# One Mish activation in bursts of four FFN groups, attention's small operations on DVE, and an engine order written by hand from the third unit on

## The chip, the cores and the metric

The kernel runs on one core of a Trainium2 chip. The core has a matrix engine (PE, whose weight loads are shown as PEld), a vector engine (DVE), an activation engine (ACT), a general engine (POOL) and a queue engine (SP) that issues the DMAs here. The metric is device time in microseconds (us); the time of a kernel is the median over its runs. The profile is of one execution, and its span runs from the first to the last instruction.

## The reference

Queries, keys and values have the shape 4 batches x 8 heads x 768 tokens x 64. Each key is compared only with queries of the same hash bucket (the signs of six projections). The attention output, as 3072 tokens x 512, goes through a feed-forward layer (FFN) with the Mish activation.

```python
mask = q_bucket[:, :, :, None] == k_bucket[:, :, None, :]
scores = scale * np.matmul(q, k.transpose(0, 1, 3, 2))
scores = np.where(mask, scores, -1000000000.0)
scores = scores - np.max(scores, axis=-1, keepdims=True)
attn = np.exp(scores)
attn = attn / (np.sum(attn, axis=-1, keepdims=True) + 1e-09)
...
h = x @ w_in                      # 512 -> 2048
sp = np.where(h > 20.0, h, np.log1p(np.exp(np.minimum(h, 20.0))))
g = h * np.tanh(sp)               # Mish
return (g @ w_out).astype(np.float32)   # 2048 -> 512
```

## The kernel before, in words

Every operand of a matmul is held as two float16 parts, a high and a low one, each scaled by a power of two; a product is three matmuls (high x high, high x low, low x high). The weights come as 64-bit floats and are taken apart on the chip.

The work goes by *units* of 256 tokens of one batch, three to a batch, twelve in all. A unit has eight *slots* of attention (`n` = 0 to 95): one pair of heads (`j`, or `hh` for one head of it) and 128 of the tokens. It also has eight *groups* of the FFN (`m` = 0 to 95): 256 hidden columns each. Group `m` is worked on 10 slots behind slot `n` (`OFF`).

A slot runs through `att_scores` (8 matmuls `ps`, both heads in PSUM, two tiles in all), `att_max` (DVE, negated maximum of each head), `att_scale` (POOL: `sc`, then `bi`), `att_exp` (ACT, two exponentials `p` with their sums; three `p` tiles in all), `att_recip` (POOL `rt`, DVE reciprocal `rv`), `att_hi` (POOL, high part of the normalised weights, tile `hl`, three in all), `att_lo` (DVE, low part, then an SP DMA that transposes `hl` into `PTt`). Every second slot has `att_pv` (36 matmuls `pv`, the product with V) and `att_x` (high part on ACT, low part on DVE, into `X`).

A group runs through `ffn_h` (24 matmuls into `h`), `ffn_a` (ACT: a scaled copy `hs`, an exponential), `ffn_m` (DVE minimum), `ffn_r` (ACT: square, logarithm, exponential), `ffn_g` (DVE), `ffn_g2` (POOL, high and low part) and `ffn_out` (12 matmuls into two sums `o`, one for each 128 tokens). After the eighth group the sums are copied out and stored. `h`, `pv` and the small hash and statistics matmuls share two PSUM tiles (`acc`).

In the last unit of a batch the next batch's keys and values are loaded, split, hashed and transposed; every unit does that for the next unit's queries (`kvL`, `kvS`, `kvM`, `kvK`, `kvH`, `kvV`, and `q` in their place: load, square sum, scale, split, hash, values).

Until slot 25 a scheduler orders the instructions of each engine by a model of their times. From slot 26 on (`MAN0`) each engine follows the program's order, which a string sets, one letter for a step. S is scores, x maximum, c scale, E exponentials, C reciprocal, I and 0 and 1 the high and low parts; H, A, M, R, G, g, O are the FFN's steps, V and X the product with V:

```python
OFF, STEP0, STEP1 = 10, 'SCxgIH0cAV1GEMXORP', 'SCxgIH0cAV1GEMXOmhsRklP'
LAGS = (0, 0, 0, 0, 1, 1, 1, 1, 0, 0, 0, 0, 1, 2, 2)
```

Of the kernel before, what the change touches and what calls it, by code (L numbers as in the profile page):

```python
# [29 lines left out]
def lsh_attention_mish_ffn(  # L30
# [31 lines left out]
    nc.scalar.preload_act_table_set("natural_log_exp_and_others")  # L62

# [738 lines left out]
```

## Time and profile before

| what | value |
|---|---|
| runs shown | 988.99 us median of 3 (987.65 to 990.5) |
| profiled execution: span | 984.3 us, 17525 instructions |
| profiled execution: its own time | not listed apart; the median stands 4.7 us above the span |
| PE busy | 814.6 us (83%) |
| DVE busy | 704.6 us (72%) |
| POOL busy | 704.1 us (72%) |
| ACT busy | 685.1 us (70%) |
| mean granted PE clock | 0.956 |

Rows with `|` are groups: line, engine, operation, output<-input, shapes and count, then busy us and mean ns of one, then the idle time of the engine ahead of them and who ended it. `x<-y` with a name behind the arrow is a wait: the instruction on the left waited for the one on the right, with us in total, times and the longest. Rows that begin with two numbers are a start and a duration in us. A row `A:B` gives each engine's busy time in that stretch. In a row with three numbers and slashes these are the least, the median and the largest ns. Matmuls are pipelined: the next starts before the last has ended, so PE's work is read from start to start.

### The profile page before, as it was taken

What the parts mean: (1) busy time and instruction counts of PE and PEld (TensorE: products, weight loads), DVE (VectorE), ACT (ScalarE), POOL (GpSimd) and SP (SyncE); (2) the same over time, 40 slices, a digit from 0 to 9 for tenths busy, and PEclk for the clock granted to TensorE, in tenths of its full rate; (3) what the DMA queues carried; (4) which work ended last, traced back from release to release, by engine and by line L of the source; (5) the groups of instructions that cost most, each with busy time, mean ns of one, the idle gap of its engine ahead of it and who ended that gap; (6) DMA issues with size and microseconds to landing.
All of it is one profiled execution on the core that took longest, in us unless ns stands there. A gap on an engine that the chain in (4) does not pass through costs nothing.

```text
span 984.3 us, 17525 instructions
## 1 busy us (share of the span) xinstructions
PE 814.6 (83%) x6470; PEld 530.7 (54%) x6470; DVE 704.6 (72%) x1169; ACT 685.1 (70%) x1136; POOL 704.1 (72%) x793
## 2 busy tenths in 40 slices
PE   1254567678878999999788999998889999999997
PEld 0132245355545666666455666665555666666664
DVE  5769968897687777776777777777776777777421
ACT  4646778656756867778675778687677677777674
POOL 3589978867777776767887767768886767676522
PEclk9996679889999999999999999999999999999999
DMA  7998695465886655567796565667975555544200
GB/s 216 285 217 189 192 220 163 99 134 103 172 168 132 151 119 124 134 158 182 165 187 130 132 149 129 130 162 168 178 177 134 124 130 128 126 106 119 65 23 22
DMA packets 432693, 143.75 MB, mean 146 GB/s; under 512 B 402912, under 2 KB 423392, under 8 KB 432608
## 3 DMA queue, kind: packets, MB, share of 16 engines
q1 hardware_dynamic: 432608, 142.65, 64.0%
q8 instruction: 50, 0.82, 0.4%
q14 instruction: 35, 0.29, 0.1%
HBM read 35.65 MB, written 6.29 MB: 43 GB/s over the span
## 4 chain that ended last, share of the span: by engine, by line
POOL 39%; issue 15%; PE 13%; ACT 10%; DVE 7%; DMA 3%; POOLq 0%; SPq 0%; ACTq 0%; DVEq 0%
POOL hl L470 11%; POOL ffb L566 7%; POOL sv L437 7%; ACT p L445 6%; POOL sv L438 5%; POOL ffb L565 4%; POOL rt L452 2%; PE h L532 2%; PE h L533 2%; PE h L534 2%; PE o L580 2%; PE o L581 2%; PE ps L422 2%; PE o L582 2%; PE pv L501 1%
## 5 line engine op out<-in xcount | busy, mean ns | idle before, releaser
L445 ACT ACTIVATE p<-ps,sv 128x768 f32<-128x768 f32 x192 | 188.3, 984 | 109.2 <-POOL sv L438 103.2
L486 DVE SCALAR_TENSOR_TENSOR hl<-p,sv,hl 128x768 f16<-128x768 f32 x175 | 227.1, 1330 | 51.1 <-POOL hl L470 50.9
L422 PE MATMUL ps<-KT,QT 128*128 128x512 f16 (+1 forms) x768 | 165.4, 348 | 84.1 <-ACT p L445 73.8
L532 PE MATMUL h<-X,wi 128*128 128x256 f16 x768 | 212.7, 277 | 11.8 <-DVE hsum L328 5.4
L533 PE MATMUL h<-X,wi 128*128 128x256 f16 x768 | 212.4, 277 | 0.0
L534 PE MATMUL h<-X,wi 128*128 128x256 f16 x768 | 212.1, 276 | 0.0
L432 DVE TENSOR_REDUCE sv<-ps 128x1 f32<-128x768 f32 x192 | 175.7, 946 | 20.6 <-PE ps L422 20.4
L470 POOL TENSOR_SCALAR hl<-p,sv 128x768 f16<-128x768 f32 x178 | 167.6, 951 | 10.5 <-DVE sv L453 3.5
L422 PEld LDWEIGHTS <-QT 128*128 128x128 f16 x768 | 75.9, 101 | 153.9 <-issue 107.1
L580 PE MATMUL o<-wo,ffb 128*128 128x512 f16 x384 | 147.5, 384 | 9.2 <-POOL ffb L565 8.5
L582 PE MATMUL o<-wo,ffb 128*128 128x512 f16 x384 | 144.3, 380 | 6.8 <-POOL ffb L566 6.8
L581 PE MATMUL o<-wo,ffb 128*128 128x512 f16 x384 | 146.9, 382 | 0.0
L452 POOL TENSOR_SCALAR rt<-sv 128x2 f32<-128x2 f32 x96 | 38.6, 402 | 123.5 <-ACT p L445 120.3
L541 ACT ACTIVATE ffb<-h,cnegFalse 128x512 f32<-128x512 f32 x88 | 60.1, 684 | 90.8 <-PE h L534 85.9
L566 POOL TENSOR_TENSOR ffb<-ffb 128x512 f16<-128x512 f32 x96 | 113.3, 1181 | 7.7
L501 PE MATMUL pv<-PTt,VT 128*64 128x256 f16 x1728 | 110.0, 281 | 6.0 <-DMA PTt<-hl 5.5
L437 POOL TENSOR_SCALAR sv<-sv,sig 128x2 f32<-128x2 f32 x96 | 93.9, 978 | 21.3 <-DVE sv L432 17.3
L501 PEld LDWEIGHTS <-VT 128*64 128x64 f16 x1728 | 94.7, 113 | 19.6 <-issue 14.1
L565 POOL TENSOR_SCALAR ffb<-ffb 128x512 f16<-128x512 f32 x96 | 63.7, 663 | 45.3 <-DVE ffb L558 31.8
L533 PEld LDWEIGHTS <-wi 128*128 128x128 f16 x768 | 76.3, 99 | 25.0 <-issue 13.7
L532 PEld LDWEIGHTS <-wi 128*128 128x128 f16 x768 | 76.3, 99 | 20.7 <-issue 1.9
L558 DVE SCALAR_TENSOR_TENSOR ffb<-ffb 128x512 f32<-128x512 f32 x96 | 66.6, 694 | 23.4 <-ACT ffb L553 23.4
(217 smaller groups left out, 1287.3 us busy)
## 6 DMA issues: line engine op xcount, KB each, us to landing
out_dram<-ffb SPq DMA_DIRECT2D x24, 256.0 KB, 2.1
stg<-in_k_dram SPq DMA_DIRECT2D x12, 384.0 KB, 3.9
stg<-in_v_dram SPq DMA_DIRECT2D x12, 384.0 KB, 4.3
stg<-in_q_dram SPq DMA_DIRECT2D x9, 512.0 KB, 4.7
wo<-in_moe_w_out_dram SPq DMA_DIRECT2D x8, 512.0 KB, 4.7
wi<-in_moe_w_in_dram SPq DMA_DIRECT2D x7, 512.0 KB, 4.1
PTt<-hl SPq DMA_TRANSPOSE x192, 3.4
stg<-in_moe_w_in_dram SPq DMA_DIRECT2D x5, 512.0 KB, 6.2
```

The costliest lines, as they stand in the source:

```text
L422: nc.tensor.matmul(ps[:, c0 * P:c1 * P], QT[u][:, sl, qi], KT[b, j][:, sl, hh * NCH + c0:hh * NCH + c1].rearrange("p c t -> p (c t)"), sta ...
L432: nc.vector.tensor_reduce(out=d["mneg"][:, hh:hh + 1], in_=d["ps"][hh][:, :S], axis=AX.X, op=ALU.max, negate=True)
L445: nc.scalar.activation(pt, d["ps"][hh][:, :S], AF.Exp, bias=d["bi"][:, hh:hh + 1], scale=d["sc"][:, hh:hh + 1], accum_out=d["sm"][:, hh:hh ...
L470: nc.gpsimd.tensor_scalar(out=hl[:, 0], in0=d["p"][hh], scalar1=rv, scalar2=1.0, op0=ALU.mult, op1=ALU.mult)
L486: nc.vector.scalar_tensor_tensor(out=hl[:, 1], in0=d["p"][hh], scalar=d["rv"][:, hh:hh + 1], in1=hl[:, 0], op0=ALU.mult, op1=ALU.subtract)
L501: nc.tensor.matmul(pv[hh * D:(hh + 1) * D, 0:256], vt[:, w, hh * NCH + c], pt[:, hh, a * NCH + c].rearrange("p s t -> p (s t)"), start=(x ...
L532: nc.tensor.matmul(o, wh, X[:, 0, c], start=(c == 0), stop=False)
L533: nc.tensor.matmul(o, wh, X[:, 1, c], start=False, stop=False)
L534: nc.tensor.matmul(o, wl, X[:, 0, c], start=False, stop=(c == NCC - 1))
L566: nc.gpsimd.tensor_tensor(out=g[:, 1], in0=d["hs"], in1=g[:, 0], op=ALU.subtract)
L580: nc.tensor.matmul(OB[u][s], gh, wo[:, g, 0, f2], start=first, stop=False)
L581: nc.tensor.matmul(OB[u][s], gh, wo[:, g, 1, f2], start=False, stop=False)
```

## The change

The FFN's activation becomes one ACT pass with the Mish function, `ffn_mish`, straight from PSUM. Mish and the exponential lie in different activation tables, so that ACT needs a table load between them. The program now goes by *blocks* of four slots and four groups: in each block the four groups' `ffn_h` and `ffn_mish` come as a burst, and then the four slots' exponentials. There are 44 loads in ACT's order: one at the start, and two in each of 21 blocks, and one for the last burst. The FFN now follows 12 slots behind (`LAG` of three blocks). Its high part is a POOL pass (`ffn_hi`) and its low part a DVE pass (`ffn_lo`). `sc`, `bi` and `rt` move from POOL to DVE. From slot 12 on one of a slot's two high parts moves from POOL to ACT (`lo_pool` 5). The order of each engine is the program's from block 6 on, which is slot 24. The stores get a step of their own (`ffn_store`), and the casts ahead of the statistics matmuls too (`kvD`, `qD`, `bD`). The first unit's groups are summed in two segments instead of three.

```diff
-    nc.scalar.preload_act_table_set("natural_log_exp_and_others")
+    nc.scalar.preload_act_table_set("exp_and_others")
...
+    def act_set(kind, ins):
+        other = latest.get("mish" if kind == "exp" else "exp")
+        if other is not None and not manual[0]:
+            tc.add_manual_dep(ins.ins, other.name,
...
-        nc.gpsimd.tensor_scalar(out=d["sc"], in0=d["mneg"], scalar1=HALF, scalar2=d["sg"], op0=ALU.is_le, op1=ALU.mult)
-        nc.gpsimd.tensor_tensor(out=d["bi"], in0=d["mneg"], in1=d["sc"], op=ALU.mult)
+        nc.vector.tensor_scalar(out=d["sc"], in0=d["mneg"], scalar1=HALF, scalar2=d["sg"], op0=ALU.is_le, op1=ALU.mult)
+        nc.vector.tensor_tensor(out=d["bi"], in0=d["mneg"], in1=d["sc"], op=ALU.mult)
...
-        nc.gpsimd.tensor_scalar(out=t, in0=d["sm"], scalar1=1e-9, scalar2=2.0 ** -PT, op0=ALU.add, op1=ALU.mult)
+        nc.vector.tensor_scalar(out=t, in0=d["sm"], scalar1=1e-9, scalar2=2.0 ** -PT, op0=ALU.add, op1=ALU.mult)
...
+            if lo_pool(n, hh) == 5:
+                nc.scalar.activation(hl[:, 0], d["p"][hh], AF.Copy, scale=rv)
...
-    def ffn_a(m):
-        u, g = divmod(m, NG)
-        ps = FB[m]["ps"]
-        hs, t = ffb[:, ring(m)], ffb[:, 3 + ring(m)]
-        nc.scalar.activation(hs, ps, AF.Copy, scale=CNEG[u == 0][:, g:g + 1])
-        nc.scalar.activation(t, hs, AF.Exp, scale=ES[u // NU, u == 0][:, g:g + 1])
...
-        nc.vector.tensor_scalar(out=t, in0=t, scalar1=E20, scalar2=None, op0=ALU.min)
...
-        nc.scalar.activation(t, t, AF.Square, bias=one_c)
-        nc.scalar.activation(t, t, AF.Ln, bias=one_c)
-        nc.scalar.activation(t, t, AF.Exp, bias=ln2_c, scale=-1.0)
...
+    def ffn_mish(m):
         d = FB[m]
+        d["m"] = ffb[:, m % 3]
+        act_set("mish", nc.scalar.activation(d["m"], d["ps"], AF.Mish, scale=HS[d["key"]][:, d["g"]:d["g"] + 1]))
...
+    def ffn_hi(m):
...
+        nc.gpsimd.tensor_scalar(out=d["p"][:, 0], in0=d["m"], scalar1=GS[d["key"]][:, d["g"]:d["g"] + 1], scalar2=1.0,
+                                op0=ALU.mult, op1=ALU.mult)
...
+    def ffn_lo(m):
...
+        nc.vector.scalar_tensor_tensor(out=d["p"][:, 1], in0=d["m"], scalar=GS[d["key"]][:, d["g"]:d["g"] + 1],
+                                       in1=d["p"][:, 0], op0=ALU.mult, op1=ALU.subtract)
...
-    MAN0 = 26
...
+    LAG = 3
+    MAN0 = 6
...
+    def block(blk):
+
+        n, m = 4 * blk, 4 * (blk - LAG)
...
+        pv(2 * blk - 2)
+        ffn(ffn_h, 0)
+        tail(-1)
+        ffn(ffn_mish, 0)
+        ffn(ffn_h, 1)
+        lows(-1)
+        ffn(ffn_hi, 0)
+        ffn(ffn_mish, 1)
+        head(0)
+        ffn(ffn_lo, 0)
+        prep(n, "mh")
+        ffn(ffn_h, 2)
...
+        ffn(ffn_h, 3)
+        ffn(ffn_hi, 2)
+        ffn(ffn_mish, 3)
+        ffn(ffn_lo, 2)
+        exps(0)
+        prep(n, "skdlP")
+        ffn(ffn_hi, 3)
+        ffn(ffn_out, 0, 0)
+        ffn(ffn_out, 0, 1)
+        ffn(ffn_out, 1, 0)
+        for x in range(1, 4):
+            tail(x - 1)
+            head(x)
+            exps(x)
+            if x == 1:
+                ffn(ffn_lo, 3)
+            lows(x - 1)
+            if x == 2:
+                pv(2 * blk - 1)
+            prep(n + x, "mhskdlP")
+            if x == 1:
+                ffn(ffn_out, 1, 1)
+                ffn(ffn_out, 2, 0)
+                ffn(ffn_out, 2, 1)
+            elif x == 2:
+                ffn(ffn_out, 3, 0)
+            else:
+                ffn(ffn_out, 3, 1)
```

In a block, `tail(x)` is reciprocal and high parts of slot x, `lows(x)` its low parts, `head(x)` scores, maximum and scale; -1 is the last slot of the block before. An output is now given in halves, `ffn_out(group, 128 tokens)`, six matmuls each.

ACT in the middle of the kernel before; `p` is an exponential, `h` an FFN group, `X` the attention output:

```order
L510 ACTIVATE X_5843<-pv_6473,xf_5672 128x256
L551 ACTIVATE ffb_86<-ffb_86,one_c_76 128x512
L552 ACTIVATE ffb_86<-ffb_86,one_c_76 128x512
L553 ACTIVATE ffb_86<-ffb_86,ln2_c_78 128x512
L541 ACTIVATE ffb_86<-h_6559,cnegFalse_2038 128x512
L542 ACTIVATE ffb_86<-ffb_86,es_5676 128x512
L445 ACTIVATE p_6593,sv_6547<-ps_6537,sv_6547 128x768
L445 ACTIVATE p_6595,sv_6547<-ps_6542,sv_6547 128x768
```

and ACT in a block of the changed kernel, from the last slot's exponentials on (`hl` is a high part):

```order
L458 ACTIVATE p_9213,sv_9208<-ps_9198,sv_9208 128x768
L458 ACTIVATE p_9215,sv_9208<-ps_9203,sv_9208 128x768
L524 ACTIVATE X_8823<-pv_9228,xf_7872 128x256
L474 ACTIVATE hl_9297<-p_9215,sv_9208 128x768
L550 ACT_TABLE_LOAD
L550 ACTIVATE ffb_82<-h_9267,hs_7876 128x512
L550 ACTIVATE ffb_82<-h_9300,hs_7876 128x512
L550 ACTIVATE ffb_82<-h_9349,hs_7876 128x512
L550 ACTIVATE ffb_82<-h_9377,hs_7876 128x512
L458 ACT_TABLE_LOAD
L458 ACTIVATE p_9405,sv_9343<-ps_9333,sv_9343 128x768
L474 ACTIVATE hl_9433<-p_9407,sv_9343 128x768
```

Five passes of a group between two slots' exponentials have become four Mish passes between two table loads, and a high part stands ahead of the next slot's exponentials.

DVE for one slot of the kernel before; the names are those of the steps above:

```order
L453 RECIPROCAL sv_5924<-rt_6019 128x2
L432 TENSOR_REDUCE sv_6018<-ps_6008 128x1
L432 TENSOR_REDUCE sv_6018<-ps_6013 128x1
L486 SCALAR_TENSOR_TENSOR hl_6026<-p_5970,sv_5924,hl_6026 128x768
L486 SCALAR_TENSOR_TENSOR hl_6028<-p_5972,sv_5924,hl_6028 128x768
L558 SCALAR_TENSOR_TENSOR ffb_86<-ffb_86 128x512
L547 TENSOR_SCALAR ffb_86<-ffb_86 128x512
L511 SCALAR_TENSOR_TENSOR X_5843<-pv_6062,xf_5672,X_5843 128x256
```

and for one slot of a block of the changed kernel:

```order
L465 TENSOR_SCALAR rt_4470<-sv_4429 128x2
L466 RECIPROCAL sv_4429<-rt_4470 128x2
L428 TENSOR_SCALAR sig_4477<-HKV_1918,hqf_3934 128x1
L447 TENSOR_REDUCE sv_4489<-ps_4479 128x1
L447 TENSOR_REDUCE sv_4489<-ps_4484 128x1
L452 TENSOR_SCALAR sv_4489<-sv_4489,sig_4477 128x2
L453 TENSOR_TENSOR sv_4489<-sv_4489 128x2
L500 SCALAR_TENSOR_TENSOR hl_4473<-p_4434,sv_4429,hl_4473 128x768
L500 SCALAR_TENSOR_TENSOR hl_4475<-p_4436,sv_4429,hl_4475 128x768
L525 SCALAR_TENSOR_TENSOR X_3805<-pv_4502,xf_2854,X_3805 128x256
```

Three 128x2 operations have come to DVE, two of them between the maxima and the low parts, and the FFN's two passes have gone from this place.

More of the change, by code (lines that the diff above doesn't have):

```diff
@@ L515, in lsh_attention_mish_ffn @@
     FB, OB = {}, {}
-    SEGS = ((0, 4), (4, 6), (6, NG))
-    accs = [ffb[:, 2], ffb[:, 5]]
-    def ring(m):
-        return m % 2 if m < NG + 2 else (m - NG) % 3
+    SEGS = ((0, 4), (4, NG))
     def ffn_h(m):
@@ L596, in lsh_attention_mish_ffn @@
-    TOT_U = B * NU
-    MAN0 = 26
-    OFF, STEP0, STEP1 = 10, 'SCxgIH0cAV1GEMXORP', 'SCxgIH0cAV1GEMXOmhsRklP'
-    STEP2 = 'SCxgIH0cAV1GEMXOmhsRklP'
-    LAGS = (0, 0, 0, 0, 1, 1, 1, 1, 0, 0, 0, 0, 1, 2, 2)
-    QAT, QAL, KAT = (0, 3, 4, 4, 6), (1, 2, 4, 5, 6), (0, 1, 2, 2, 3, 3)
-    plan, pre = {}, {}
+        if g == g0 and s == 0:
+            OB[u] = [ps_o.tile([P, 512], F32, tag=f"o{x}", name=f"o{x}") for x in range(2)]
+        gt = FB[m]["p"]
+        for f2 in range(2):
+            gh = gt[:, 0, f2 * 256 + s * P:f2 * 256 + (s + 1) * P]
+            gl = gt[:, 1, f2 * 256 + s * P:f2 * 256 + (s + 1) * P]
+            first, last = (g == g0 and f2 == 0), (g == g1 - 1 and f2 == 1)
+            nc.tensor.matmul(OB[u][s], gh, wo[:, g, 0, f2], start=first, stop=False)
+            nc.tensor.matmul(OB[u][s], gh, wo[:, g, 1, f2], start=False, stop=False)
+            nc.tensor.matmul(OB[u][s], gl, wo[:, g, 0, f2], start=False, stop=last)
@@ new lines, in ffn_out, with ffn_store @@
+        if g == g1 - 1:
+            ob = ffb[:, 7 + s]
+            sc = OS[(b, u == 0), g0]
+            if g0 == 0:
+                nc.scalar.activation(ob, OB[u][s], AF.Copy, scale=sc)
+            else:
+                nc.vector.scalar_tensor_tensor(out=ob, in0=OB[u][s], scalar=sc, in1=ob, op0=ALU.mult, op1=ALU.add)
+    def ffn_store(u):
+        b, cpair = divmod(u, NU)
+        for s in range(2):
+            dst = out[b * S:(b + 1) * S].rearrange("(p c) e -> p c e", c=NCH)[:, 2 * cpair + s]
+            nc.sync.dma_start(dst, ffb[:, 7 + s])
@@ L639, in lsh_attention_mish_ffn, with bD @@
     hxs = {}
+    def bD(b):
+        batch_cast(b)
     def bS(b):
@@ new lines, in lsh_attention_mish_ffn, with pv, ffn, head @@
+    NA = TOT_U * SLOTS
+    NM = TOT_U * NG
+    def block(blk):
+        n, m = 4 * blk, 4 * (blk - LAG)
+        def pv(p):
+            if 0 <= p < NA // 2:
+                att_pv(*divmod(p, NPAIR))
+                att_x(*divmod(p, NPAIR))
+        def ffn(f, x, *a):
+            if 0 <= m and m + x < NM:
+                f(m + x, *a)
+        def head(x):
+            if n + x < NA:
+                att_scores(n + x)
+                att_max(n + x)
+                att_scale(n + x)
+        def exps(x):
+            if n + x < NA:
+                for hh in range(2):
+                    att_exp(n + x, hh)
+        def tail(x):
+            if 0 <= n + x < NA:
+                att_recip(n + x)
+                for hh in range(2):
+                    att_hi(n + x, hh)
+        def lows(x):
+            if 0 <= n + x < NA:
+                for hh in range(2):
+                    att_lo(n + x, hh)
+        pv(2 * blk - 2)
[10 more added lines that the diff above has]
+        ffn(ffn_h, 2)
+        ffn(ffn_hi, 1)
+        ffn(ffn_mish, 2)
+        ffn(ffn_lo, 1)
+        ffn(ffn_h, 3)
[24 more added lines that the diff above has]
+                ffn(ffn_out, 3, 0)
+            else:
+                ffn(ffn_out, 3, 1)
@@ L772, in lsh_attention_mish_ffn @@
+    for blk in range(NBLK + LAG):
+        if blk == MAN0:
+            manual[0] = True
+            ctx.enter_context(tc.manual_schedule())
+        block(blk)
+    for n in sorted(plan):
+        prep(n, "P")
     assert not plan, plan.keys()
```

208 lines of the change are left out of this document (87 added, 121 removed).

## Prediction

> **What bounds the kernel now.** I read, in this order: the engines' busy time by stage, the chain of work that ended last, the matrix engine's (PE's) timeline inside one quiet stretch, and then the costs and waits of the operations that the change touches. The rows by stage are: units 0 to 2 with the weights' preparation, units 3 to 11, the tail of FFN alone, and of the middle stage one unit that also prepares the next batch (434 to 511) and one that does not (369 to 434).
>
> ```profile
> core 0: us, PE busy (x) PEld busy (x) DVE busy (x) ACT busy (x) POOL busy (x), PEclk, DMA share, GB/s
> 0.00:300.00 300.00, 181.12 (x1353) 111.41 (x1354) 234.36 (x415) 191.68 (x314) 227.59 (x224) 0.89 0.76 181
> 300.00:914.00 614.00, 570.25 (x4684) 378.78 (x4683) 452.09 (x728) 450.58 (x759) 452.51 (x543) 0.99 0.64 141
> 914.00:984.30 70.30, 63.25 (x440) 40.50 (x436) 18.16 (x29) 42.86 (x63) 24.02 (x28) 1.00 0.14 38
> 434.00:511.00 77.00, 67.50 (x562) 43.68 (x560) 56.83 (x95) 57.78 (x101) 62.76 (x70) 0.98 0.80 182
> 369.00:434.00 65.00, 63.03 (x516) 42.13 (x514) 48.08 (x73) 48.58 (x82) 45.89 (x58) 1.00 0.57 130
> ```
>
> The reader is to see that no single engine bounds all of it. In the quiet unit PE is busy 63.0 of 65 us. In the unit with preparation PE loses 9.5 us and POOL is the next busiest (62.8 of 77). In the first 300 us PE works 181 us only, and DVE (234) and POOL (228) carry the stage. All the PE idle time there is: 119 us early, 44 us in the middle, 7 us in the tail. The work of PE is not changed, so the change can win no more than these.
>
> The chain of work that ended last gives the starts of slots and units:
>
> ```profile
> 300.32 2.06 ACT p L445 x4
> ...
> 349.90 1.77 POOL hl L470 x2
> ...
> 357.79 1.77 POOL hl L470 x2
> ...
> 434.19 2.06 ACT p L445 x4
> ...
> 511.14 2.05 ACT p L445 x4
> ...
> 645.63 2.06 ACT p L445 x4
> ...
> 722.34 2.06 ACT p L445 x4
> ...
> 914.63 2.13 issue
> ```
>
> A quiet slot lasts 7.89 us (349.90 to 357.79), so four take 31.5. Slot 24 starts at 300.3, the last one's exponentials at 914.6. Units 5 and 8, with a batch's preparation, last 76.95 and 76.7 us; the pairs 3+4 and 6+7 last 133.9 and 134.5.
>
> PE's own rows in a quiet slot, one after the other: a product with V, the first of 12 matmuls of FFN output, the 8 scores, the first of 24 of FFN hidden, the next output:
>
> ```profile
> 358.97 2.15 PE L501 MATMUL pv<-PTt,VT 128*64 128x256 f16 x36
> 361.06 0.39 PE L580 MATMUL o<-wo,ffb 128*128 128x512 f16 x1
> ...
> 363.66 1.46 PE L422 MATMUL ps<-KT,QT 128*128 128x512 f16 x8
> 364.96 0.27 PE L532 MATMUL h<-X,wi 128*128 128x256 f16 x1
> ...
> 367.58 0.38 PE L580 MATMUL o<-wo,ffb 128*128 128x512 f16 x1
> ```
>
> From start to start: pv 2.09, output 2.60, scores 1.30, hidden 2.62. Four slots need 4 x (2.60 + 1.30 + 2.62) + 2 x 2.09 = 30.3 us of PE, and take 31.5. In quiet stretches there are 1.2 us in four slots to be had, no more, whatever ACT, DVE and POOL save.
>
> **The change, part by part.** Durations of what is removed, added or moved, and the waits that the change aims at (the last two rows are of the first 300 us):
>
> ```profile
> L437 POOL TENSOR_SCALAR sv<-sv,sig 128x2 f32<-128x2 f32 x96 | 93.9, 978 | 21.3 <-DVE sv L432 17.3
> L438 POOL TENSOR_TENSOR sv<-sv 128x2 f32<-128x2 f32 x96 | 65.4, 682 | 7.3
> L470 POOL TENSOR_SCALAR hl<-p,sv 128x768 f16<-128x768 f32 x178 | 167.6, 951 | 10.5 <-DVE sv L453 3.5
> L565 POOL TENSOR_SCALAR ffb<-ffb 128x512 f16<-128x512 f32 x96 | 63.7, 663 | 45.3 <-DVE ffb L558 31.8
> L566 POOL TENSOR_TENSOR ffb<-ffb 128x512 f16<-128x512 f32 x96 | 113.3, 1181 | 7.7
> L432 DVE TENSOR_REDUCE sv<-ps 128x1 f32<-128x768 f32 x192 | 175.7, 946 | 20.6 <-PE ps L422 20.4
> L453 DVE RECIPROCAL sv<-rt 128x2 f32<-128x2 f32 x96 | 15.4, 160 | 41.3 <-POOL rt L452 39.7
> L486 DVE SCALAR_TENSOR_TENSOR hl<-p,sv,hl x175: 999/1018/2871, 74.6 to 921.4; 128x768 f16<-128x768 f32 x175
> L558 DVE SCALAR_TENSOR_TENSOR ffb<-ffb x96: 667/678/2059, 155.7 to 975.1; 128x512 f32<-128x512 f32 x96
> L547 DVE TENSOR_SCALAR ffb<-ffb 128x512 f32<-128x512 f32 x96 | 46.6, 485 | 24.5 <-ACT ffb L542 24.4
> L541 ACT ACTIVATE ffb<-h,cnegFalse 128x512 f32<-128x512 f32 x88 | 60.1, 684 | 90.8 <-PE h L534 85.9
> L552 ACT ACTIVATE ffb<-ffb,one_c 128x512 f32<-128x512 f32 x96 | 69.2, 721 | 2.9
> L463 ACT ACTIVATE hl<-p,sv 128x768 f16<-128x768 f32 x7 | 6.5, 922 | 0.0
> L501 PE MATMUL pv<-PTt,VT 128*64 128x256 f16 x1728 | 110.0, 281 | 6.0 <-DMA PTt<-hl 5.5
> 980.27 0.69 ACT L587 ACTIVATE ffb<-o,os 128x512 f32<-128x512 f32 x1 [0.62 <-PE o L582]
> 0.71 1.28 ACT L62 ACT_TABLE_LOAD   x1 [0.71 <-PEq L786]
> 3.57 0.21 ACT L114 ACTIVATE tok<-pj 128x6 bf16<-128x6 f32 x1 [1.57 <-DMA pj<-in_proj_dram]
> PTt<-hl SPq DMA_TRANSPOSE x192, 3.4
> PE ps L422 <- ACT p L445: 51.1, 20, 9.6
> ACT p L445 <- POOL sv L438: 39.6, 19, 6.3
> ```
>
> *Mish.* Five ACT passes a group (one of 0.68, four near 0.72, 96 groups) become one. I price the one as the old first pass, which also reads PSUM with a scale: 0.68. It adds table loads, two in each of 21 bursts and one more. The only load in the trace takes 1.28 us; the next instruction starts 1.57 us after it, and the row puts that gap down to a DMA, so a switch costs 1.28 at least and 2.85 at most. I take 1.28, because the row names another cause for the rest. The Trainium skill has two pages on this: "ScalarE: Activation LUTs", What ACT_TABLE_LOAD costs, adds a drain of about 1.38 us to a load of 1.283, while "ScalarE activation tables: per-element evaluation and per-set limits", its opening part, puts two sets one load of 1283 ns apart. The row has the 1.28 of both; the drain no row here shows. By the first page a burst's return to the exponential costs 1.38 us more, and 18 of them 25 us.
>
> *Small operations.* `sc` and `bi` leave POOL, where a 128x2 operation takes 0.98 and 0.68. On DVE the nearest row is the reciprocal, also 128x2: 0.16. With one waiting for the other I take 0.2 each; the ends are 0.16 and POOL's 0.98. `rt` moves too: 0.2, with the reciprocal 0.3.
>
> *Weights' high and low halves.* One of two high halves moves from POOL to ACT (0.92 each); the FFN low half moves from POOL to DVE, by the ratio of widths 512/768 of 1.02 us about 0.74 with its overhead, in place of two DVE passes (0.68 and 0.49). POOL keeps one FFN pass of 0.66 and loses that of 1.18.
>
> *Stores and small moves.* The output's two stores are issued some slots behind their copies instead of at once, so SP no longer stands at them ahead of the transposes. I cost this at nothing: PE waited 5.5 us for transposes in the whole run, and were they later by that much, the block's walk would show it at pv. Casts set ahead of their matmuls, two sums in place of three in unit 0 and the other scales are small DVE operations, inside the early stage's range.
>
> *The block of four slots* (units 3 to 11 hold 18). I walk it from the end of the last hidden matmul of the burst, at 0. The fourth Mish ends at 0.85, the table load at 2.1, the two exponentials of slot 0 at 3.1 and 4.2. PE meanwhile does three half outputs, 3.9, then scores of slot 1 (each head 0.65): no wait. Reciprocal, both maxima (1.8) and scales on DVE end at 6.9; the first exponential at 7.95. The second needs a `p` tile that the first low half frees: FFN low 0.74 and low 1.02 on DVE, 8.7, so it ends at 9.7. Scores of slot 2 start on PE at 9.1, second head 9.75: no wait. DVE's next scales end at 12.3, but ACT stands at the moved high half: its tile is the third of three, and free only when the transpose of slot 0's first head has landed, 8.7 + 3.4 = 12.1. With 0.92 on top the exponentials run 13.0 to 15.1. PE, done with pv and a half output at 13.8, waits for them in slot 3's scores, which end at 15.7 in place of 15.1. Then a half output, pv, two hidden, scores, two hidden: 15.2 us, and the next block starts at 30.9. The load ahead of the next burst is done near 23 and the first Mish is needed at 25.6, so it is hidden. 30.9 against 31.5 is 0.6 a block: 18 x 0.6 = 11 us gained.
>
> *Preparation in the middle.* Over quiet units (64.9 us: 133.9 of units 3+4 less what follows a preparation), units 5 and 8 cost 12 us more each, units 3, 6 and 9 some 4 to 6. Of these 39 us part is PE's own (9.5 of unit 5's 77 us are idle) and part is POOL. POOL is now nearly free (1.66 of scales, 1.18 of FFN and 0.95 of a high half go, per slot), but DVE's preparation now stands in the same queue as the scales. I take a fifth, 8 us; the ends are 30 and a loss of 10.
>
> *The first 300 us* keep a scheduler. ACT stood 39.6 us waiting for `bi` on POOL, 19 times, and PE 51.1 for ACT. The path from maximum to exponential gets 1.66 - 0.4 = 1.26 us shorter in 24 slots, 30 us if each stood on the path; but DVE, the busiest there, takes the operations. I take half: 15. Ends: 45 (all of the 39.6 and POOL's relief) and a loss of 12 (24 slots x 0.6 of new DVE work, less what FFN takes off it).
>
> *Tail.* FFN now lags 12 slots in place of 10. From the last exponential PE has 1.3 + 2.09 + 62.6 + 2.09 still to do less the 2 us by which it is ahead, and 4.6 for copy and store (984.3 - 980.27 and the 0.6 ahead): 70.7 against 984.3 - 914.6 = 69.7: a loss of 1.
>
> **Sum.** 984.3 - 11 - 8 - 15 + 1 = 951.3 of span. The median shown, 988.99, lies 4.7 above this profile's span; the same on top gives 956.
>
> **Rivals.**
> - *More comes back (925).* With DVE freed of POOL's interference (a low half takes 1.02 at the median and 2.87 at worst) the preparation fits beside PE: 25 in place of 8, and early 30 in place of 15, 32 below the forecast. The Trainium skill, "SBUF — State Buffer", SBUF: two separate sides, has POOL and a DVE operation with two SBUF inputs shut each other out; 0.98 us for 128x2 on POOL agrees. Against it: DVE is in order, and its queue gets longer.
> - *Table switches cost twice (984).* At 2.85 the exponentials of slot 0 end 1.57 later, and little between there and slot 3's scores has slack: 18 x 1.57 = 28 us. For it speaks only the gap of 1.57 behind the load, which the row gives to a DMA.
> - *DVE's queue becomes the bound (1000).* In slots 1 to 3 one DVE turn (0.3 + 1.8 + 0.4 + 2.04, and up to 0.74 of FFN) is 4.5 to 5.3 us beside 5.2 and 4.7 of PE. If `sc` and `bi` on DVE cost nearer POOL's 0.98, or each hand-over 0.3, a turn grows by 1.2; two turns a block wait on it: 2.4 x 18 = 43 us. Beyond 0.9 us a turn the change is slower than before. For it: two dependent operations and a high half now stand ahead of every exponential. Against: 0.16 for the reciprocal.
> - *Nothing is gained (988).* Quiet slots are PE's already, and if the early stage hangs on its weights' DMAs (share 0.76) only the 11 us are left, and preparation takes them.
>
> **How the numbers follow.** The forecast has 0.40, the larger gain 0.20, dearer table switches 0.13, DVE's queue 0.21, nothing 0.06. About 0.3%, 3 us, can be told from no change here. Faster: the first three, less a little of the third, and a little of the last: 0.72; same 0.06; slower 0.22. The range runs from the larger gain to the DVE rival, 925 to 1003; the forecast's own range, by the ends of preparation and early stage taken half way, is 936 to 976.
>
> **What would show it.** In the profile after: POOL's busy time near 310 to 340 in place of 704, ACT near 550, DVE about as before; table loads in 43 places, each followed by the next ACTIVATE within 0.2 us; a Mish of 0.68; quiet units of 63 to 65 us, units 5 and 8 nearer 72 to 75; slot 24 starting near 285. Wrong would be: ACT idle ahead of the exponentials with DVE as releaser, PE's scores waiting more than 1 us in each block, a gap of 1.4 us behind each table load, or slot 24 at 300 or later.

## The result: 7.4% slower

| | before | after |
|---|---|---|
| median us (range, runs) | 989.75 (987.65 to 990.99, 4) | 1063.18 (1059.79 to 1064.54, 4) |
| ratio to before, 95% interval | | 1.0744 [1.0718, 1.0769] |
| profiled span us, mean granted clock | 984.3, 0.956 | 1057.8, 0.92 |

Predicted were 956 (925 to 1003). The stages of the changed kernel, cut where slot 24's and the last slot's exponentials begin, then unit 5 (with a batch's preparation) and unit 4 (quiet):

```profile
core 0: us, PE busy (x) PEld busy (x) DVE busy (x) ACT busy (x) POOL busy (x), PEclk, DMA share, GB/s
0.00:319.80 319.80, 189.85 (x1379) 116.63 (x1380) 237.25 (x452) 177.22 (x280) 153.14 (x128) 0.83 0.76 171
319.80:986.90 667.10, 575.79 (x4590) 378.22 (x4588) 431.42 (x866) 361.99 (x577) 169.51 (x185) 0.95 0.69 130
986.90:1057.80 70.90, 66.97 (x503) 45.87 (x503) 13.19 (x19) 16.18 (x25) 9.25 (x13) 0.99 0.16 38
462.50:557.20 94.70, 71.41 (x559) 46.04 (x558) 53.42 (x112) 48.89 (x80) 26.57 (x28) 0.87 0.70 139
394.10:462.50 68.40, 62.87 (x516) 42.39 (x515) 45.90 (x88) 38.93 (x62) 14.65 (x17) 1.00 0.68 128
```

Beside before's bounds (300.3, 914.6, 984.3) the 73.5 us of span are 19.5 early, 52.7 in the middle and 1.2 in the tail. POOL has shed 372 us, ACT 130, and no stage is shorter. Units, from exponential to exponential, for the kernels that matter below:

| unit | 3 | 4 | 5 | 6 | 7 | 8 | 9 | 10 |
|---|---|---|---|---|---|---|---|---|
| before | 69.0 | 64.9 | 77.0 | 69.6 | 64.9 | 76.7 | 71.2 | 65.0 |
| after | 74.3 | 68.4 | 94.7 | 73.5 | 68.1 | 93.4 | 73.9 | 68.3 |
| e1, preparation spread | 76.9 | 74.4 | 77.2 | 80.9 | 70.5 | 76.4 | 78.3 | 68.5 |
| e16, Mish first | 72.7 | 66.0 | 93.5 | 73.8 | 65.1 | 96.0 | 73.2 | 66.0 |
| e7, one pass, slot by slot | 66.8 | 61.4 | 68.9 | 63.9 | 61.4 | 71.0 | 62.8 | 61.4 |
| e12, Mish, slot by slot | 68.5 | 62.8 | 74.8 | 69.0 | 63.1 | 75.2 | 68.9 | 62.7 |
| e17, all mended | 72.3 | 73.0 | 74.4 | 75.8 | 71.9 | 76.4 | 75.2 | 66.1 |

The groups of the changed kernel that the prediction had priced, and the transposes with their median time to landing:

```profile
L550 ACT ACTIVATE ffb<-h,hs 128x512 f32<-128x512 f32 x96 | 65.2, 687 | 156.9 <-PE h L544 156.6
L550 ACT ACT_TABLE_LOAD x22 | 28.2, 1283 | 0.4
L458 ACT ACT_TABLE_LOAD x21 | 26.9, 1283 | 0.4
L474 ACT ACTIVATE hl<-p,sv 128x768 f16<-128x768 f32 x84 | 78.5, 935 | 120.0 <-DMA PTt<-hl 66.1 <-DVE sv L453 25.2 <-DVE sv L466 11.2
L452 DVE TENSOR_SCALAR sv<-sv,sig 128x2 f32<-128x2 f32 x96 | 27.2, 284 | 2.7
L453 DVE TENSOR_TENSOR sv<-sv 128x2 f32<-128x2 f32 x96 | 22.6, 236 | 2.9
PTt<-hl SPq DMA_TRANSPOSE x192, 4.1
```

The prices hold, or nearly: Mish 0.69 us, a load 1.28, `sc` and `bi` 0.28 and 0.24. What is new is ACT's 66 us ahead of the moved high half, waiting for transposes, which land in 4.1 us where it was 3.4. PE's waits from 320 to 1000 us name the places:

```profile
PE hp L334 <- DMA KT<-tok: 35.2, 9, 6.4
PE pv L515 <- DMA PTt<-hl: 31.7, 27, 2.1
PE hp L334 <- DVE X L525: 10.3, 2, 6.6
PE ps L437 <- ACT p L458: 7.5, 21, 1.4
```

PE stands 45.5 us at hash projections (`hp`), 36 of it in units 5 and 8 and the rest in the units that follow a preparation, and 31.7 at products with V. A block in unit 10, on PE and then on ACT (the burst's last hidden matmul ends at 864.0, the next block's at 898.1):

```profile
878.57 0.81 PE L437 MATMUL ps<-KT,QT 128*128 128x512 f16 x4 [0.45 <-ACT p L458]
...
882.96 0.30 PE L515 MATMUL pv<-PTt,VT 128*64 128x256 f16 x1 [1.32 <-DMA PTt<-hl]
884.22 2.15 PE L515 MATMUL pv<-PTt,VT 128*64 128x256 f16 x35 [0.95 <-DMA PTt<-hl]
```

```profile
876.61 0.94 ACT L474 ACTIVATE hl<-p,sv 128x768 f16<-128x768 f32 x1 [2.85 <-DMA PTt<-hl]
...
883.02 0.94 ACT L474 ACTIVATE hl<-p,sv 128x768 f16<-128x768 f32 x1 [2.59 <-DMA PTt<-hl]
883.87 0.97 ACT L458 ACTIVATE p<-ps,sv 128x768 f32<-128x768 f32 x1
...
888.76 0.94 ACT L474 ACTIVATE hl<-p,sv 128x768 f16<-128x768 f32 x1 [0.88 <-DVE sv L466]
889.71 1.28 ACT L550 ACT_TABLE_LOAD   x1
891.01 1.43 ACT L550 ACTIVATE ffb<-h,hs 128x512 f32<-128x512 f32 x2
```

The high half of slot 2 waits for a transpose (883.02) and holds the exponentials of slot 3 behind it. PE stands at the product with V of slots 0 and 1: the two transposes of slot 1 were issued at 877.43 and 878.95 and landed at 882.92 and 884.17, after 5.5 and 5.2 us. The next burst's Mish comes at 891.0, behind the last slot's high half and a load.

### The profile page after: what moved, and what is told of

The parts are those of the page before. It is cut to its first block, busy times and chain, and to the rows that moved or that the text cites. A ratio compares the mean times of both kernels' runs of the same rounds, so it can differ in the third digit from the quotient of the medians.

```text
span 1057.8 us, 17062 instructions
## 1 busy us (share of the span) xinstructions
PE 832.6 (79%) x6470; PEld 540.7 (51%) x6470; DVE 681.9 (64%) x1337; ACT 555.4 (53%) x879; POOL 331.9 (31%) x325
## 5 line engine op out<-in xcount | busy, mean ns | idle before, releaser
L458 ACT ACTIVATE p<-ps,sv 128x768 f32<-128x768 f32 x192 | 188.4, 984 | 76.5 <-DVE sv L453 60.9
L484 POOL TENSOR_SCALAR hl<-p,sv 128x768 f16<-128x768 f32 x94 | 93.1, 991 | 380.2 <-DVE sv L466 185.8
L500 DVE SCALAR_TENSOR_TENSOR hl<-p,sv,hl 128x768 f16<-128x768 f32 x175 | 180.0, 1054 | 42.8 <-POOL hl L484 32.7
L515 PE MATMUL pv<-PTt,VT 128*64 128x256 f16 x1728 | 122.1, 294 | 37.7 <-DMA PTt<-hl 33.0
L575 PE MATMUL o<-wo,ffb 128*128 128x512 f16 x384 | 151.1, 393 | 0.0
L576 PE MATMUL o<-wo,ffb 128*128 128x512 f16 x384 | 151.0, 393 | 0.0
L574 PE MATMUL o<-wo,ffb 128*128 128x512 f16 x384 | 150.7, 393 | 0.0
L550 ACT ACTIVATE ffb<-h,hs 128x512 f32<-128x512 f32 x96 | 65.2, 687 | 156.9 <-PE h L544 156.6
L474 ACT ACTIVATE hl<-p,sv 128x768 f16<-128x768 f32 x84 | 78.5, 935 | 120.0 <-DMA PTt<-hl 66.1
L437 PEld LDWEIGHTS <-QT 128*128 128x128 f16 x768 | 78.3, 103 | 122.5 <-issue 70.3
L555 POOL TENSOR_SCALAR ffb<-ffb,gs 128x512 f16<-128x512 f32 x96 | 71.9, 752 | 202.4 <-ACT ffb L550 197.2
L560 DVE SCALAR_TENSOR_TENSOR ffb<-ffb,gs 128x512 f16<-128x512 f32 x96 | 81.3, 853 | 71.7 <-POOL ffb L555 71.7
L543 PEld LDWEIGHTS <-wi 128*128 128x128 f16 x768 | 76.2, 99 | 19.4 <-issue 9.5
L542 PEld LDWEIGHTS <-wi 128*128 128x128 f16 x768 | 76.3, 99 | 16.2 <-issue 5.3
L544 PEld LDWEIGHTS <-wi 128*128 128x128 f16 x768 | 76.2, 99 | 9.9
L576 PEld LDWEIGHTS <-ffb 128*128 128x128 f16 x384 | 38.6, 101 | 48.1 <-issue 5.9
(205 smaller groups left out, 891.0 us busy)
```

The source lines that it names most:

```text
L437: nc.tensor.matmul(ps[:, c0 * P:c1 * P], QT[u][:, sl, qi], KT[b, j][:, sl, hh * NCH + c0:hh * NCH + c1].rearrange("p c t -> p (c t)"), sta ...
L458: act_set("exp", nc.scalar.activation(pt, d["ps"][hh][:, :S], AF.Exp, bias=d["bi"][:, hh:hh + 1], scale=d["sc"][:, hh:hh + 1], accum_out=d ...
L484: nc.gpsimd.tensor_scalar(out=hl[:, 0], in0=d["p"][hh], scalar1=rv, scalar2=1.0, op0=ALU.mult, op1=ALU.mult)
L500: nc.vector.scalar_tensor_tensor(out=hl[:, 1], in0=d["p"][hh], scalar=d["rv"][:, hh:hh + 1], in1=hl[:, 0], op0=ALU.mult, op1=ALU.subtract)
L515: nc.tensor.matmul(pv[hh * D:(hh + 1) * D, 0:256], vt[:, w, hh * NCH + c], pt[:, hh, a * NCH + c].rearrange("p s t -> p (s t)"), start=(x ...
L542: nc.tensor.matmul(o, wh, X[:, 0, c], start=(c == 0), stop=False)
```

## The experiments

Each is the changed kernel or the kernel before with the edit shown; times are medians, ratios are to the kernel before, run beside it on the same chip (986.85 to 989.45). Most have two runs and an interval of some 5 us to either side: smaller differences between them are not told apart.

**e1: the preparation spread** (units 5 and 8; the new batch's scales come two slots later too).

```diff
-            for f, x in zip((kvL, kvS, kvD, kvM, kvK, kvH, kvV), KAT): at(base + 2 * j + x, f, b, j)
+  KSP = ((0,2,2,3,3,4,4), (3,4,4,5,5,7,6), (5,7,7,8,8,10,8), (8,10,10,11,11,12,11))   # at(base + KSP[j][i]), b > 1
+  QSP = (-2, -1, -1, 0, 0, 2)                                                         # queries of units 6 and 9
```

> The changed kernel with another timetable of slots for the preparation of batches 2 and 3 (units 5 and 8) alone: the queries of the coming unit are split at the start of the unit, and each key/value pair's split, hash projection and next squares stand one to two slots further apart; work and engines are the same. Theory 1 (the short slots of a block bring a hash projection too soon after the split whose transpose it reads, and PE stands there in its written order): the waits at hp in units 5 and 8 (21.8 us in unit 5) go, these units fall from 94.7 and 93.4 us to about 78, the span from 1057.8 to about 1025. Theory 2 (table switches are what is lost) and theory 3 (the small operations on DVE are): no wait is removed that matters, the time stays within 5 us of 1063.

1046.09 us, ratio 1.0585 [1.0538, 1.0631], 17 less. Units 5 and 8 fall to 77.2 and 76.4, as expected; PE's hash projections there no longer wait:

```profile
480.42 0.56 PE L334 MATMUL hp<-pj,QT 128*128 128x12 f16 x16
...
497.49 0.45 PE L334 MATMUL hp<-pj,KT 128*128 128x12 f16 x12
```

But units 4, 6, 7 and 9, into which the steps were spread, take 2 to 7 us more each: of the 35 us saved in units 5 and 8 these give 20 back. Theory 1 has the place right, not the net worth.

**e2: the product with V behind two hidden groups.**

```diff
-        pv(2 * blk - 2)          # ahead of ffn(ffn_h, 0)
+        pv(2 * blk - 2)          # behind ffn(ffn_h, 1), from slot 24 on
```

> The changed kernel with the first product with V of a block written behind the block's second hidden group in place of ahead of its first, from slot 24 on; nothing else. In a quiet unit PE idles 2.3 us a block at that product, for the transposes of slot 1. Theory 1 (transposes come late for PE's written order): that wait goes, a quiet block falls from 34.2 to about 32, quiet units from 68.3 to about 64, the whole by 18 x 2.3 = 40 us or somewhat less, to about 1025. Theory 2 (table switches): PE then waits for the exponentials behind the load in place of the transposes, a quiet block stays within 1 us of 34.2, the whole within 15 us of 1063.

1112.42 us, ratio 1.1256 [1.1206, 1.1306]: 49 slower, against both theories. The product now needs the PSUM tile of the burst's first group, which is Mish's to free, and Mish stands behind the last slot's high half: PE waited 60.1 us there ("PE pv <- ACT ffb"). The wait at V was one end of a longer chain.

**e3: no table switch** (a scaled copy in place of Mish; the nonlinearity is left out).

```diff
-  AF.Mish, scale=HS[...]
+  AF.Copy, scale=HS[...]
```

> The changed kernel with a scaled copy on ScalarE in place of Mish (the nonlinearity is left out), so that no table has to be switched; all else as it is. Theory 1 (late transposes and projections): the 42 loads of 1.28 us are 54 us of ACT, but only the one ahead of a block's first exponential stands on the chain to the transposes, and there the written order of PE waits anyway: the time falls by 21 x 0.6 to 21 x 1.3, 13 to 27 us, to 1036 to 1050. Theory 2 (table switches are the loss): it falls by 50 us and more, to 1010 or less. Theory 3 (small operations on DVE): within 10 us of 1063.

1060.95 us, 1.0735 [1.0682, 1.0789]: 2.2 us less without the 43 loads, which is inside the spread of the runs (1059.31 and 1062.58 here, 1059.79 to 1064.54 there). Theory 2 falls, and theory 1's 13 to 27 was too much as well: without the load slot 0's exponentials come 1.4 us sooner, slot 1's wait that much longer (for DVE), and the block is as long.

**e4: the small operations back on POOL.**

```diff
-        nc.vector  (sc, bi, rt)
+        nc.gpsimd
```

> The changed kernel with sc, bi and rt back on POOL, all 96 slots; nothing else. Theory 3 (their place on DVE costs): the time falls, by 20 us or more. Theory 1: the path from maximum to exponential gets 1.66 - 0.4 = 1.26 us longer, and rt to reciprocal about 0.8, in every slot; PE's waits grow, by about 2 us in each of 96 slots where nothing covers it: 1063 becomes 1090 to 1200. Theory 2: within 10 us of 1063.

1079.48 us, 1.0923 [1.0804, 1.1042]: 16 slower. In the blocks their place on DVE is a gain, by less than theory 1 reckoned. Theory 3 falls for the middle; slot 24 starts at 317.4 against 319.8, which is no clear difference (below, at e11).

**e5: all high halves on POOL.**

```diff
-        return 5 if hh else 0
+        return 0
```

> The changed kernel with all high halves of the weights on POOL from slot 12 on (the one moved to ACT goes back). In the changed kernel ACT stands 66 us at the moved high half for a transpose that has to free its buffer, with the next exponentials behind it. Theory A (that in-order wait on ACT delays the exponentials, and so the last transposes ahead of the product with V): POOL takes the wait instead, where nothing stands behind it but the next half; a quiet block falls from 34.2 to about 32.5, the whole by 25 to 35 us, to about 1030 to 1040. Theory B (the block is set by its burst and by the chain scores, maxima, exponentials, halves, transposes of three slots in a row, whoever makes the half): within 10 us of 1063.

1067.66 us, 1.0787 [1.0722, 1.0852]: within 5 us, as theory B has it. ACT's 66 us at that half are not a cause by themselves.

**e6, e7, e8: the kernel before with parts of the change**: small operations on DVE; one copy in place of five passes; both.

```diff
-        nc.gpsimd  (sc, bi, rt)                                    # e6, e8
+        nc.vector
-        nc.scalar.activation(t, hs, AF.Exp, ...)                   # e7, e8; and min, Square, Ln, Exp
-        nc.vector.scalar_tensor_tensor(out=d["hs"], ...)           # e7, e8
-        nc.gpsimd.tensor_tensor(out=g[:, 1], in0=d["hs"], in1=g[:, 0], op=ALU.subtract)
+        nc.vector.scalar_tensor_tensor(out=g[:, 1], in0=d["hs"], scalar=one_c, in1=g[:, 0], ...)
```

> The kernel before with sc, bi and rt on DVE in place of POOL; nothing else of the change. From the run of the changed kernel with these back on POOL (16 us slower) their place on DVE is a gain where POOL's 1.66 us stand between maxima and exponentials. In the kernel before quiet slots are PE's already, so the gain is early and in the units with preparation: 988 becomes 965 to 982. Rival (DVE's queue becomes the bound): 995 or more.

> The kernel before, slot by slot in its own order, with one scaled copy on ACT in place of its five passes (the nonlinearity is left out), no DVE passes for it, the FFN's high half on POOL and its low half on DVE as in the changed kernel; no bursts, no table switch, small operations on POOL. It gives what the saved work is worth without the blocks of four. Theory 1 (the new order loses, the saved work gains): 988 becomes 950 to 975. Theory 4 (the saved work was off the critical path, so nothing could be gained): 983 to 990.

> Both of the two before together: the kernel before with one pass in place of five (nonlinearity left out) and sc, bi and rt on DVE, in its old order slot by slot. It is the changed kernel's work without its order and its table switches. Theory 1: 935 to 960, some 100 to 125 us less than the changed kernel, all of which is then the price of the order. Theory 4: 975 to 990.

e6: 993.02 us, 1.0042 [1.0025, 1.0059]. Quiet units gain 2.3 us (62.7), but slot 24 comes at 322.5 in place of 300.3: a slight loss, where a gain was expected. e7: 932.11, 0.9417 [0.9363, 0.9472], more than theory 1 hoped. Its middle and its unit 4:

```profile
293.50:862.70 569.20, 551.95 (x4665) 376.08 (x4665) 396.68 (x659) 253.82 (x476) 356.53 (x469) 0.99 0.71 152
...
360.30:421.60 61.30, 61.30 (x516) 42.09 (x514) 41.50 (x65) 26.30 (x50) 34.57 (x49) 1.00 0.65 138
```

PE is busy all of a quiet unit. The saved work is worth 57 us slot by slot, 45 of them in the middle (614.3 to 569.2). e8: 958.75, 0.9686 [0.9615, 0.9758]; the small operations on DVE cost 27 of it. e3 does about the same work without switches in blocks, and takes 1060.95: 102 us stand between them, for the order with what belongs to it (lag of 12, stores and casts as steps of their own, a high half on ACT, which e5 found to be worth little). Of the 102, 11 have been lost by slot 24 (315.6 against 304.6).

**e9, e10, e12: real Mish slot by slot** (172 table loads in the trace, 10 slots' lag, sums and stores placed to fit).

```diff
-    block(blk)                      # four slots, four groups
+    for op in 'SCxgIH0cV1EXOmhsdRklP': ...    # one slot; R = ffn_mish(m) behind E
     e9, e12: sc, bi, rt, all high halves on POOL; e10: as in the changed kernel
     g = ffn_hi, ffn_lo of group m - 1 in e9 and e10, of m - 2 in e12
```

> The changed kernel's Mish, FFN halves and stores in the slot order of the kernel before: one group a slot, lag of 10 slots, one Mish behind the two exponentials of each slot with a table load on either side (192 loads, 246 us of ACT in place of 54), hand-written order from slot 26, sc, bi and rt on POOL, all high halves of the weights on POOL. All of the reference is computed. Theory 1 (the blocks of four are the loss, switches are cheap where ACT has room): in the run with one pass and no switch a quiet unit had 26.3 us of ACT in 61.3, and 8 x 2.56 = 20.5 more fit; the time is 932 + 0 to 30, so 932 to 962, faster than the kernel before and over 100 us faster than the changed kernel. Theory 2 (each switch in the chain costs its load): 96 x 1.28 to 96 x 2.56 more than 932, 1055 to 1180.

> The same with sc, bi, rt on DVE and one of two high halves on ACT, as the changed kernel places them: the changed kernel's work, placement and Mish, with the order alone put back (and 150 more table loads). Theory 1: as the run before with 27 us more for the small operations on DVE in this order, as they cost between the two runs with one pass: 960 to 990. Theory 4 (placement, not order, is the loss): 1030 or more.

1071.61 us, 1.0858 [1.0811, 1.0904], and 1089.40, 1.103 [1.0977, 1.1082]. Both missed. POOL in e9 says why:

```profile
405.16 0.69 POOL L555 TENSOR_SCALAR ffb<-ffb,gs 128x512 f16<-128x512 f32 x1 [2.17 <-ACT ffb L550]
405.83 2.22 POOL L484 TENSOR_SCALAR hl<-p,sv 128x768 f16<-128x768 f32 x2
408.04 0.97 POOL L452 TENSOR_SCALAR sv<-sv,sig 128x2 f32<-128x2 f32 x1
409.10 0.75 POOL L453 TENSOR_TENSOR sv<-sv 128x2 f32<-128x2 f32 x1
```

POOL waits for a Mish behind the last exponentials, with the scales of the next exponentials queued behind it: a chain of 9 us a slot. In e10 the chain is as long and passes through DVE: the FFN's low half waits for POOL's high half, which waits for Mish, and the scales stand behind it in DVE's queue.

```profile
415.63 1.38 DVE L560 SCALAR_TENSOR_TENSOR ffb<-ffb,gs 128x512 f16<-128x512 f32 x1 [0.34 <-POOL ffb L555]
```

e12 cuts the chain of e9 by a lag of one more slot (e10 was not run with it):

> As the run with one Mish and two table loads a slot, sc, bi, rt and the high halves on POOL, with one edit: a group's high and low half are made two slots behind its hidden matmuls, as the kernel before does, in place of one. In that run POOL stood at the FFN's high half 13.7 us a unit for a Mish that follows the exponentials, with sc and bi of the next slot behind it: exponentials, load, Mish, high half, scales, exponentials made one chain of 9 us a slot. Theory 1 (the loads themselves fit beside the rest): the chain is cut, quiet units fall from 74 to 61 to 64 us, the time from 1072 to 932 plus 0 to 25, 932 to 957, under the kernel before. Theory 2 (192 loads cost in themselves): 1030 or more.

**977.06 us, 0.9896 [0.987, 0.9922]: 1% faster than the kernel before, 8% than the changed one.** The same POOL operations, with nothing to wait for:

```profile
394.20 0.69 POOL L555 TENSOR_SCALAR ffb<-ffb,gs 128x512 f16<-128x512 f32 x1
394.87 1.78 POOL L484 TENSOR_SCALAR hl<-p,sv 128x768 f16<-128x768 f32 x2
396.71 0.71 POOL L452 TENSOR_SCALAR sv<-sv,sig 128x2 f32<-128x2 f32 x1
```

One lag is worth 94.6 us. Small operations and high halves are on POOL here; in the blocks each of these places alone brought nothing (e4, e5). The time missed its range from above: quiet units are as expected (62.7 to 63.1), but slot 24 comes at 308.2 against 293.5 in e7, and units 5, 6, 8 and 9 take 4 to 6 us more than there.

**e11, e15: the first 24 slots slot by slot**, e15 with `sc`, `bi`, `rt` on POOL there.

```diff
-    block(blk)                              # blk < 6
+    slot(n, 4 * LAG)                        # n < 24; blocks from slot 24 on
```

> The changed kernel with its first 24 slots, those that the scheduler still orders, written slot by slot in the order of the kernel before (FFN from slot 12, one Mish with two table loads a slot there); blocks of four from slot 24 on as they are. Theory 5 (blocks written ahead of the scheduler cost the early 20 us): slot 24 starts near 300 in place of 319.8, the time falls by about 20, to 1043. Theory 6 (the small operations on DVE cost the early part: with these alone the kernel before reached slot 24 at 322.5 in place of 300.3): slot 24 stays at 315 to 330, the time within 8 us of 1063.

> The changed kernel with its first 24 slots written slot by slot and their sc, bi and rt on POOL; blocks of four as they are from slot 24 on. If the early loss is order and placement together: the slots up to 23 take as long as in the kernel before (slot 23 starts near 285 to 290, against 300.2 in the changed kernel and 295.1 with the order alone), the change-over to blocks costs some 15 more, the time is 1045 to 1055. If neither is the cause, slot 23 stays at 295 or later.

1066.00 us, 1.0793 [1.0739, 1.0846], and 1059.94, 1.0735 [1.0696, 1.0774]. Slot 23's first exponential, in the changed kernel, in e11 and in e15 (287.55 in the kernel before):

```profile
300.18 0.97 ACT L458 ACTIVATE p<-ps,sv 128x768 f32<-128x768 f32 x1
```

```profile
295.10 0.99 ACT L458 ACTIVATE p<-ps,sv 128x768 f32<-128x768 f32 x1
```

```profile
288.58 0.99 ACT L461 ACTIVATE p<-ps,sv 128x768 f32<-128x768 f32 x1
```

Order and placement together bring back all but 1 us of the 12.6 lost by slot 23; the order alone brings 5.1. The 1.2 of the placement alone (e4, 298.96) is no clear gain: with the same first 24 slots as the changed kernel, e1, e2, e13, e14 and e16 start slot 23 between 298.6 and 302.7. Slot 23 itself takes 23 to 27 us in these two kernels, against 19.6 in the changed kernel and 12.8 in the kernel before, so the total hardly moves. In it the order changes over to blocks; no run takes that apart.

**e13, e14, e16, e17: the blocks mended.** The product with V behind the fourth hidden group and the half outputs spread (e13); with e1's timetable (e14); e13 with the first Mish ahead of the last high half (e16); e16 with e1's timetable and e15's early slots (e17).

```diff
-        pv(2 * blk - 2)                     # first in the block
+        att_pv(...)                         # behind ffn(ffn_h, 3); outputs 2 behind scores 2, 3 behind scores 3
-        tail(-1); ffn(ffn_mish, 0)
+        ffn(ffn_mish, 0); tail(-1)          # e16, e17
```

> The changed kernel with PE's order in a block changed from slot 24 on: the block's first product with V stands behind the fourth hidden group (where Mish has already freed its PSUM tile and the transposes of slot 1 have had 10 us more), and the half outputs are spread so that the scores of slots 1 to 3 keep their places. Theory 1: the wait of 2.3 us at that product goes and nothing takes its place; a quiet block falls from 34.2 to 31 to 32, the whole by 18 x 2 to 3 us, 36 to 54, to 1010 to 1027. Theory B (the chain of three slots' scores, maxima, exponentials and halves behind the burst sets the block): a quiet block stays over 33.5, the whole over 1050.

> The same with the wider timetable of the preparation of batches 2 and 3, which alone gave 17 us. Theory 1: the two add, 17 us less than the run before it: 990 to 1012, still slower than the kernel before, by what the first 24 slots lose. If the shared cause is another, the sum is under 10 us.

> The block with the product with V behind the burst (as in e13) and, on ACT, the burst's first table load and Mish ahead of the last slot's high half in place of behind it, from slot 24 on. In e13 that high half started at 897.0, 2.2 us behind the last exponential, and Mish at 899.3, with its group ready at 894. Theory B (the chain of four slots' attention and then the burst, one behind the other on ACT and DVE, sets the block): the block gets shorter by what is taken from between, 2 to 3 us, quiet units from 70 to 64 to 66, the whole by 35 to 55 us against e13, to 1012 to 1032. If something else holds the block, under 10 us.

> The same with the wider timetable of the preparation of batches 2 and 3, and the first 24 slots slot by slot with sc, bi and rt on POOL there: all that was found against the changed kernel at once, the blocks of four and their 42 table loads from slot 24 on kept. If the causes found are the causes: e14 gave 1040; less 30 for the block's chain, less 4 early: 1000 to 1015. If the sum is under 30 us below e14, one of them has been mistaken.

e13: 1067.04 us, 1.0807 [1.0767, 1.0846]. The wait at V is gone, and PE stands at the burst instead:

```profile
PE hp L334 <- DMA KT<-tok: 30.0, 6, 6.9
PE h L542 <- ACT ffb L550: 19.5, 13, 3.9
PE hp L334 <- DVE hx L100: 18.0, 3, 6.0
```

This fits theory B: the last slot's attention, then the load and Mish, follow one another on ACT. e16 shortens just that: 1048.09, 1.0592 [1.0539, 1.0646], 19 less than e13; quiet units take 65.1 to 66.0, in their range. The second block of unit 10 takes 31.2 us, but the first 34.9: there ACT has a square sum of the next queries and two output copies ahead of the load and Mish, PE waits for Mish, and 15 matmuls run at half the clock.

```profile
885.85 0.16 PE L98 MATMUL st<-sb,ones 128*128 128x1 bf16 x1 [1.08 <-ACT ffb L550]
887.25 0.37 PE L542 MATMUL h<-X,wi 128*128 128x256 f16 x1 [1.21 <-ACT ffb L550]
887.20:890.20 3.00, 2.95 (x15) 2.09 (x15) 2.93 (x7) 0.00 (x0) 0.94 (x1) 0.50 0.95 175
```

The total missed its range, since units 5 and 8 did not move (93.5, 96.0). e14: 1039.64, 1.0529 [1.049, 1.0568], 27 under e13 (17 expected). e17: 1019.29, 1.0301 [1.0248, 1.0354], 20 under e14 where 25 to 40 were expected: by its own test one of the causes was mis-sized. Of the 73 us lost, the causes found give back 44. The other 30 lie in two places of e17's trace: slot 23 starts at 287.65, as in the kernel before, but takes 25.2 us in place of 12.8, and units 3 to 11 take 20 us more than in the kernel before, with the largest rises, 6 to 8 us each, in units 4, 6 and 7. PE's longest waits there are at hidden matmuls, for Mish (14.5 us) and for the next queries' statistics (12.2). What makes the change-over long, and what each wait is worth, stays open.

## Why the prediction was wrong, point by point

- *Prices*: right for Mish, loads and the high half, near for the small operations (0.28 and 0.24 against 0.2 each) and the FFN's low half (0.85 against 0.74). The landing of 3.4 us was taken over from the kernel before, and was 4.1 in the median and 5.5 and 5.2 for the two transposes that PE waited for in the block shown.
- *Block of four* (-11): the walk was right up to slot 3's scores, which end at 16.2 us of the block against 15.7. The step that failed is the next one, "Then a half output, pv, two hidden, scores, two hidden": it followed PE alone, though the part on stores had said that late transposes would show "at pv". By the walk's own numbers slot 1's last low half ends near 14.3 and its transpose lands at 17.7, 0.7 behind PE; with 5.2 in place of 3.4 PE stood there for 2.3 us, and the block took 34.2 in place of 30.9. ACT reached Mish at 27.0, not by 25.6, which PE did not feel in this block. e16, in another order of PE, removes the wait at pv: its quiet blocks take 31 to 35 us. The measure was off as well: 31.5 is four times one slot of 7.89, while a quiet unit of 64.9 makes 32.5 for four, and e7 gained 3.6 us a quiet unit where the prediction allowed 2.4. The four quiet units 4, 7, 10 and 11 lost 6 us together (11, with one burst fewer ahead of its last slot, gained 3.8).
- *Preparation* (-8): units 3, 5, 6, 8 and 9 lost 46.5. The step "POOL is now nearly free" counted engines' load. Nothing was walked past the written order: split and hash projection are one slot apart as before, but three of four slots had become 5 to 7 us long instead of 8, shorter than a key's split (0.95 us on POOL, 1.30 on DVE), transpose (4.0) and the queues ahead of them. PE stood at `hp`; e1 takes these waits away, though only 17 us of the time with them.
- *First 300 us* (-15): +19.5. "I take half" had the wrong sign. On the busiest engine there, DVE, the small operations cost 22 us by themselves in the old order (e6); with the order they account for the 12.6 us lost up to slot 23 (e15). The other 6.9 are lost in slot 23.
- *Tail* (+1): +1.2, right.
- *Sum*: 106.5 us between 951.3 and 1057.8: 34.5 early, 54.5 preparation, 17 quiet units (the walk's 11, meant for all 18 blocks, is counted to the quiet units here).
- *Rivals*: dearer switches are excluded (e3; behind each of the 43 loads the next row starts within 0.02 us). DVE's queue as the bound (1000) came nearer in time, but not as the cause in the blocks: taking the operations off DVE made the changed kernel slower (e4). In the old order their place on DVE does cost (e6, and 27 us in e8). "More comes back" was nearest to what the saved work is worth, in an order that keeps the slots (e7, 932).
- Of what was to show it, POOL (332), ACT (555), DVE (682), 43 loads and Mish came as told; quiet units, units 5 and 8 and slot 24 at 319.8 showed it wrong. So did ACT's idle time ahead of the exponentials with DVE as releaser, 60.9 us.

## What to carry to other kernels

A change that relieves engines and rewrites the order is two changes: time the relief alone in the old order first (here 57 us gained), then each thing that is moved (here 27 us lost with the small operations), then the order (here 102 us lost). In an order written by hand, steps a fixed number of slots apart are apart only by those slots' time; when slots become uneven, recheck each step that crosses a DMA, on every engine's queue, not on the busiest alone. A wait taken away by itself (e2, e13) shows the next one; follow the chain round to where it began before pricing it.
